# Tanh pieces for GELU, one GELU buffer, whole matmuls, and pair sums added on GpSimd, in a transformer block on one core

## The chip, the core and the metric

The kernel runs on one core of a Trainium2 chip. A core has a matmul engine (TensorE, in the profile PE, with its weight loads shown apart as PEld), a vector engine (VectorE, DVE), an engine for functions such as exp (ScalarE, ACT), GpSimd (POOL) and SyncE (SP), which here issues every DMA. Matmuls write to PSUM, eight banks of 512 float32 columns over 128 partitions; everything else lies in SBUF. The metric is the device time of one execution in microseconds. Before the change it is 1161.94 us, the median of three runs (1159.34, 1161.94 and 1164.83).

## What is computed

A block of a transformer over 2048 rows of 1024 features in bfloat16: layer norm, attention with 32 heads of width 32, a residual; layer norm, a feed-forward layer of width 3584 with GELU in its tanh form, a residual.

```python
qkv = (layernorm(x) @ wqkv).reshape(B, S, 3, H, Dh).transpose(2, 0, 3, 1, 4)   # S=2048, H=32, Dh=32
scores = einsum("bhqd,bhkd->bhqk", q, k) * Dh ** -0.5
o = einsum("bhqk,bhkd->bhqd", softmax(scores), v)
h = x + o.transpose(0, 2, 1, 3).reshape(B, S, D) @ wo                          # D=1024
g = gelu(layernorm(h) @ w1 + b1, approximate=True)                             # F=3584
out = h + g @ w2 + b2
```

## The kernel before

**Tiling.** The rows are cut into eight chunks of 256 queries (qb, or u in the feed-forward part), the heads into eight groups g of four. A *job* is one chunk and one group: eight rounds, each with 256 keys. In a round, `Att.qk` (L726) lets PE make the scores of four heads (eight matmuls of 32 rows by 256 columns, L739, four side by side in the array's rows) into two of three units of two PSUM banks, and ACT turns each unit into bfloat16 exps with one instruction of 128x1024 (L749), into one of `NR` = 6 round buffers `PT` (L384). `Job.pv` (L768) multiplies them by the values (L775, eight matmuls, four side by side in the array's columns).

**Denominators.** The sums over keys come from PE too: matmuls with a matrix of ones (L804). So that they are fewer, DVE first adds the two halves of a round's exps (the *pair sum*, L790) into one of `NS` = 2 buffers `PS` (L388); seven rounds of a job go that way, the eighth directly. When a job is done, DVE copies the bank (L827), takes reciprocals (L832) and multiplies (L838) into `OT`.

**The rest for each chunk.** `wo(u)` projects the attention's output and adds the residual (L859), `ln2(u)` normalizes (its small steps on POOL, L558 to L564), `ffn1(u)` multiplies by w1 (L896, 14 blocks of 256 features), and `ffn2(u, j)` multiplies by w2 for one half j of the columns (L930). FFN1's output is taken out of PSUM with its bias by DVE (L913), into `gT`, of which there are two, one for even and one for odd chunks (L411). When all 14 blocks are there, one ACT instruction makes GELU of all 7168 columns in place (L927). `late_q` (L646) makes later chunks' Q projections from stored normalized rows, in buffers `xq` that lie over `gT`. All of these matmuls, for which scores and values leave room, are called background (`bg`).

**Narrow and whole.** `mm` (L497) writes a matmul as four narrow ones of 32 output rows, which run side by side (mode `col`, L504), or as one whole one (mode `full`, L508). Values and denominators are always `col`, scores `row`. The background beside attention is narrow, so that between two rounds of scores the array keeps its mode; the last chunk's is whole (`tail`).

**What sets the order.** Every operation is recorded as a `Task` with its engine, an estimated cost (L457 to L465: `c_act`, `c_dve`, `MM`) and the tasks it depends on through buffers. `Graph.schedule` (L108) plays them through with these costs and fixes the order on each engine; each engine then runs its list in order, and semaphores carry the dependencies (`assign`, L209). On PE, `pick_pe` (L1103) takes scores first, then values and denominators when enough rounds wait (`PV_FORCE`, `PV_START`), else background in program order. The other engines take the lowest `prio`, then program order. All DMAs are issued by SP, in the order that the same plan gives.

The program order around the change is this (L1054 to L1082):

```python
    for g in range(2):
        if g not in EXTRA:
            proj(0, g, 1, slot(), "dve")
    late_q(1, 1, [g for g in range(2, G) if g not in EXTRA])
    wo(0)
    ln2(0)
    late_q(2, 1, range(G))
    ffn1(0)
    attention(2, [g for g in range(G) if g not in EXTRA])
    for u in range(7):
        ...
            wo(u + 1)
            ln2(u + 1)
            ffn2(u, 0)
            ffn1(u + 1)
            ffn2(u, 1)
```

Behind the loop come attention's rounds that still wait, then `ffn2(6, 0)`, `wo(7)`, `ln2(7)`, `ffn2(6, 1)`, `ffn1(7)` and `ffn2(7)`, in whole matmuls but for the first.

Of the kernel before, what the change touches and what calls it, by code (L numbers as in the profile page):

```python
# [7 lines left out]
ACT = mybir.ActivationFunctionType  # L8
# [27 lines left out]

class Task:
    __slots__ = ("eng", "fns", "occ", "lat", "deps", "prio", "kind", "mode", "left", "succ", "ready", "done",
                 "order", "inc", "flow", "value", "lane", "waits", "bytes", "acq", "rel")

    def __init__(self, eng, fns, occ, lat, prio, kind, mode):
        self.eng, self.fns, self.occ, self.lat = eng, fns, occ, lat
        self.prio, self.kind, self.mode = prio, kind, mode
        self.deps = set()
        self.succ = []
        self.left = 0
        self.ready = 0.0
        self.done = None
        self.order = None
        self.inc = False  # L50
        self.flow = None
        self.value = 0
        self.lane = None
        self.waits = ()
        self.bytes = 0
        self.acq = None
        self.rel = None


class Graph:  # L60
# [145 lines left out]
        return seqs  # L206


    def assign(self, flows, lane_flows):  # L209

        for t in self.tasks:
# [101 lines left out]
def build_kernel(nc, A_x, A_wqkv, A_wo, B_w1, B_b1, B_w2, B_b2, out):  # L313
# [7 lines left out]
    DC = D // P  # L321
    FC = F // P
    SCALE = DH ** -0.5
    EPS_BF = 1.0013580322265625e-05

    x2 = A_x[0]
# [34 lines left out]
    ident, B_ident = sb(top, "ident", [P, P], BF)  # L361
    ones32, B_ones = sb(top, "ones32", [P, 32], BF)
    one_row, B_one = sb(top, "one_row", [P, P], BF)
    b2t, B_b2t = sb(top, "b2t", [P, D], BF)
    b1b, B_b1b = sb(top, "b1b", [P, FC], BF)
    b1f, B_b1f = sb(top, "b1f", [P, FC], F32)
# [14 lines left out]
    NQ = 8  # L381
    qt_lo = top.cur
    QT, B_QT = sb(top, "QT", [P, NQ, 256], BF, NQ)
    NR = 6  # L384
    pt_lo = top.cur
    PT, B_PT = sb(top, "PT", [P, NR, 2, 2, 512], BF, 2 * NR)
    pt_hi = top.cur
    NS = 2  # L388
    PS, B_PS = sb(top, "PS", [P, NS, 4, 256], BF, NS)
    ot_lo = Area(top.cur)  # L390
    OT, B_OT_ = sb(top, "OT", [P, 3, G, 256], BF, 3 * G, 2)
# [8 lines left out]
    xnT, B_xnTt = sb(ph0, "xnT", [P, 4, DC, 512], BF, 4, 4)  # L400
    Wall, B_W = sb(ph0, "Wall", [P, 6, DC, 512], BF, 6, 4)
    NXB = 4
    xb, B_xb = sb(ph0, "xb", [P, NXB, D], BF, NXB)
    NSG = 2
    stg, B_stg = sb(ph0, "stg", [P, NSG, 512], BF, NSG)


    hch, B_hch_ = sb(ffn, "hch", [P, 4, D], BF, 8)
    B_hch = [B_hch_[2 * i:2 * i + 2] for i in range(4)]
    gt_lo = Area(ffn.cur)  # L410
    gT, B_gT = sb(ffn, "gT", [P, 2, FC, 256], BF, FC)  # L411
    xq, B_xq = [], []
    for k in range(2):
        gt_lo.cur = ffn.cur - (2 - k) * FC * 512
        h, b = sb(gt_lo, "xq%d" % k, [P, DC, 512], BF)
        xq.append(h)
        B_xq.append(b)
    hnT, B_hnT = sb(ffn, "hnT", [P, DC, 256], BF, 1, 2)

    class Rings:  # L420
# [41 lines left out]
        return (62 + n / x) / 960.0 + 0.02  # L462

    def c_act(n, ap_bias=False):
        return 0.100 + (0.093 if ap_bias else 0.0) + n / 1200.0  # L465

    def pe(fns, occ, reads=(), writes=(), kind="bg", mode="full", prio=0, after=()):
        return gr.add(E.PE, fns, occ, 0.16, reads, writes, prio, kind, mode, after)
# [25 lines left out]
        if isinstance(bank, Slot):  # L494
            t.rel = bank

    def mm(bank, lhsT, rhs, start, stop, reads, narrow, cols=(0, 512)):  # L497

        c0, c1 = cols
        occ = MM * (c1 - c0) / 512.0 + 0.003  # L500
        if narrow:
            fns = []
            for j in range(4):
                fns.append(lambda p, j=j: p.matmul(psum[32 * j:32 * j + 32, bi(bank), c0:c1], lhsT[:, 32 * j:32 * j + 32], rhs,  # L504
                                                   start=start, stop=stop, tile_position=(0, 32 * j), skip_group_check=True))
            t = pe(fns, occ, reads=reads, writes=[bb(bank)], mode="col")
        else:
            t = pe(lambda p: p.matmul(psum[:, bi(bank), c0:c1], lhsT, rhs, start=start, stop=stop),  # L508
                   occ, reads=reads, writes=[bb(bank)], mode="full")
        take(t, bank)  # L510

    def act(fn, n, reads=(), writes=(), prio=0, ap_bias=False, kind="", after=()):
# [23 lines left out]
    pool(lambda g: g.memset(ones32[:], 1.0), 0.2, writes=[B_ones])  # L536
    pool(lambda g: g.memset(one_row[:], 0.0), 0.3, writes=[B_one])
    pool(lambda g: g.memset(one_row[0:1, :], 1.0), 0.3, reads=[B_one], writes=[B_one])
    pool(lambda g: g.memset(b2t[:], 0.0), 1.0, writes=[B_b2t])


    cnt = {"ln": 0, "x": 0, "sg": 0, "ps": 0, "od": 0, "q": 0}

    def layer_norm(tiles, prio, norm="dve"):

# [213 lines left out]
    class Job:  # L759
# [8 lines left out]
        def pv(self, r, s):  # L768
            g, bank, first = self.g, self.bank, self.n == 0
            last = self.n == 7  # L770
            self.n += 1
            fns = []
            for i in range(2):
                for h in range(4):
                    fns.append(lambda p, i=i, h=h: p.matmul(  # L775
                        psum[32 * h:32 * h + 32, bi(bank), 0:256], V[:, g, 2 * r + i, 32 * h:32 * h + 32],
                        PT[:, s, h // 2, h % 2, 256 * i:256 * i + 256], start=first and i == 0, stop=last and i == 1,
                        tile_position=(0, 32 * h), skip_group_check=True))
            rd = [B_PT[2 * s], B_PT[2 * s + 1], B_V[NT * g + 2 * r], B_V[NT * g + 2 * r + 1]]
            t = pe(fns, 0.224, reads=rd, writes=[self.B_O, self.B_D] if first else [self.B_O], kind="pv", mode="col")  # L780
            take(t, bank)
            while self.sums:
                self.den(*self.sums.pop(0), False)
            if r == 7 or (self.g == 0 and self.qb < 2):
                self.sums.append((s, True))
            else:
                n = cnt["ps"] % NS
                cnt["ps"] += 1
                pairs = PT[:, s, :, :, :].rearrange("p u j c -> p (u j) c")
                dve(lambda v: v.tensor_tensor(PS[:, n, :, :], pairs[:, :, 0:256], pairs[:, :, 256:512], ALU.add), c_dve(1024, 2),  # L790
                    reads=[B_PT[2 * s], B_PT[2 * s + 1]], writes=[B_PS[n]], prio=-2)
                self.sums.append((n, False))
            if last:
                while self.sums:
                    self.den(*self.sums.pop(0), not self.sums)
                self.finish()
# [99 lines left out]
    def ffn1(u, tail=False):  # L896
        R = R2 if tail else R1
        for blk in range(FC // 2):
# [4 lines left out]
                    mm(bank, R.w1[:, s, dc, f * P:(f + 1) * P], hnT[:, dc, :], dc == 0, dc == DC - 1,  # L903
                       [R.B_w1[s]] + B_hnT, not tail, (256 * f, 256 * f + 256))
            evict1(u, 2 * blk, bank, tail)
        if not tail:
            gelu(u)

    def evict1(u, fc, bank, tail):
        h = u % 2  # L910
        B_g = B_gT[h * (FC // 2) + fc // 2]
        if not tail:
            drop(dve(lambda v: v.tensor_tensor(  # L913
                gT[:, h, fc:fc + 2, :], psum[:, bi(bank), :].rearrange("p (f c) -> p f c", f=2),
                b1f[:, fc:fc + 2].unsqueeze(2).to_broadcast([P, 2, 256]), ALU.add),
                c_dve_ps(512), reads=[bb(bank), B_b1f], writes=[B_g]), bank)
        else:
            for f in range(2):
                act(lambda a, f=f: a.activation(gT[:, h, fc + f, :], psum[:, bank, 256 * f:256 * f + 256], ACT.Gelu_apprx_tanh,
                                                bias=b1f[:, fc + f:fc + f + 1], scale=1.0),  # L920
                    256, reads=[B_ps[bank], B_b1f], writes=[B_g], ap_bias=True)

    def gelu(u):
        h = u % 2
        bs = B_gT[h * (FC // 2):(h + 1) * (FC // 2)]
        g = gT[:, h, :, :].rearrange("p f c -> p (f c)")
        gr.add(E.Activation, lambda a: a.activation(g, g, ACT.Gelu_apprx_tanh, bias=0.0, scale=1.0),  # L927
               c_act(FC * 256) + 2.6, 0.14, bs, bs, -1)

    def ffn2(u, j, wide=False, W=None, banks=None):  # L930
        R = R2 if wide else R1
# [8 lines left out]
        for t in range(2):  # L940
            bank = banks[t] if banks else slot()
            tt = 2 * u + t
            hs = 2 * (u % 2) + t
            for fc in range(FC):
                s = ws[fc // 4]
                mm(bank, gT[:, u % 2, fc, t * P:(t + 1) * P], W.w2[:, s, fc % 4, :], fc == 0, False,
                   [B_gT[(u % 2) * (FC // 2) + fc // 2], W.B_w2[s]], not wide)
            mm(bank, one_row[:, :], b2t[:, c], False, True, [B_one, B_b2t], not wide)
            o = R.next("os", R.nos)
            drop(dve(lambda v, o=o, hs=hs, bank=bank: v.tensor_tensor(  # L950
                R.ost[:, o, :], psum[:, bi(bank), :], hch[:, hs, c], ALU.add),
                c_dve_ps(512), reads=[bb(bank), B_hch[hs][j]], writes=[R.B_ost[o]]), bank)
            dma(out2[tt * P:(tt + 1) * P, c], R.ost[:, o, :], P * 1024, reads=[R.B_ost[o]], prio=0)

# [102 lines left out]
    late_q(1, 1, [g for g in range(2, G) if g not in EXTRA])  # L1057
    wo(0)
    ln2(0)
    late_q(2, 1, range(G))  # L1060
    ffn1(0)
    attention(2, [g for g in range(G) if g not in EXTRA])
    for u in range(7):
        last = u == 6
        if not last:
            wo(u + 1)
            ln2(u + 1)
            ffn2(u, 0)
            ffn1(u + 1)
            ffn2(u, 1)  # L1070
        if u == 0:
            late_q(3, 0, range(G))
        if u < 5:
            attention(u + 3, range(G))
    attention_drain()
# [56 lines left out]

    num = {t: i for i, t in enumerate(gr.tasks)}
    gr.schedule(pick_pe, pool_banks)

    sems = {e: nc.alloc_semaphore(f"f_{e.name}") for e in (E.PE, E.Activation, E.DVE, E.Pool)}
    lanes = [nc.alloc_semaphore(f"f_lane{i}") for i in range(N_LANES)]
# [69 lines left out]
```

## Time and profile before

| | |
|---|---|
| median of three runs | 1161.94 us |
| the profiled execution | 1161.92 us |
| its span, first to last instruction | 1160.1 us |
| first exp of the unbroken stretch, end of the last exp | 72.4 us, 1086.0 us |
| exps (128x1024) | 1024, of them 992 in that stretch |
| GELU instructions, table loads around them | 7 of 6.18 us, 14 of 1.28 us |
| pair sums on DVE (L790) | 434 of 0.69 us |
| mean granted TensorE clock | 0.985 |

The profile is one execution. A line of a group gives the source line, engine, operation, output<-input with shapes and the number of instructions; after the first bar the group's busy time in us and the mean of one in ns (where neighbours overlap, the mean counts the overlap twice and the busy time does not); after the second the time that the engine stood idle before these instructions, with what ended it. A timeline line gives start and length in us, engine, source line, operation and number merged. "x52" on PE are single narrow matmuls, so 13 groups of four. Two shares in the middle of the run are nearly full at once: PE 94% and ACT 91% of the span; DVE is at 60% and POOL at 4%.

### The profile page before, as it was taken

The page shows a single profiled execution, that of the slowest core. Times are in us where ns is not written, and L with a number is a line of the kernel's source. Part 1 is how long each engine was busy: PE and PEld are TensorE (multiplying, and loading weights), DVE is VectorE, ACT ScalarE, POOL GpSimd, SP SyncE. Part 2 cuts the span into 40 slices and gives each one's busy share as a digit, 9 for nine tenths or more (in the row PEclk, how much of TensorE's full clock was granted, in tenths as well). Part 3 has the DMA queues.
Part 4 walks back from the last instruction along what each step waited for, and adds up shares of the span by engine and source line. Part 5 has one row for each costly group of instructions (what it writes and reads, how often), then busy time and mean ns, then how long its engine had stood idle before and what let it go on. Part 6 is the DMA issues. An engine that isn't in the chain of part 4 may idle for free.

```text
span 1160.1 us, 54760 instructions
## 1 busy us (share of the span) xinstructions
PE 1091.6 (94%) x25756; PEld 638.1 (55%) x25762; DVE 697.4 (60%) x1119; ACT 1052.5 (91%) x1096; POOL 44.4 (4%) x108
## 2 busy tenths in 40 slices
PE   8999999998998899999998999999999999887998
PEld 6655455554456456544574565466457544563484
DVE  7656676676775566467665664766476457663500
ACT  4879999999999989999999999999999999989540
POOL 3200000000100100001000000100010000000100
PEclk9999999999999999999999999999999999898999
DMA  6920200046445455646458556565576658673480
GB/s 180 233 84 3 66 20 4 3 115 207 115 139 153 132 181 167 198 142 193 131 164 256 167 166 211 150 200 153 164 230 171 206 169 247 179 208 102 145 264 19
DMA packets 265412, 174.99 MB, mean 151 GB/s; under 512 B 26849, under 2 KB 260321, under 8 KB 264418
## 3 DMA queue, kind: packets, MB, share of 16 engines
q1 hardware_dynamic: 265186, 171.48, 50.3%
q8 instruction: 202, 3.31, 1.2%
q14 instruction: 24, 0.20, 0.1%
HBM read 160.97 MB, written 10.49 MB: 148 GB/s over the span
## 4 chain that ended last, share of the span: by engine, by line
PE 66%; ACT 23%; DVE 6%; issue 2%; DMA 2%; POOL 0%; SPq 0%; DVEq 0%; POOLq 0%
PE ps L504 38%; ACT PT L749 19%; PE ps L739 11%; PE ps L775 6%; PE ps L508 6%; PE ps L804 4%; ACT gT L927 3%; DVE PS L790 2%; DVE gT L913 1%; DMA a_w2r<-in_B_w_dram 1%; PE ps L968 1%; PE ps L574 1%; DMA hch<-in_A_x_dram 1%; ACT L927 1%; DVE a_ost L950 0%
## 5 line engine op out<-in xcount | busy, mean ns | idle before, releaser
L749 ACT ACTIVATE PT<-ps 128x1024 bf16<-128x1024 f32 x1024 | 959.8, 1037 | 39.9 <-PE ps L739 34.7
L790 DVE TENSOR_TENSOR PS<-PT 128x1024 bf16<-128x1024 bf16 x434 | 289.6, 688 | 185.7 <-PE ps L804 152.6
L739 PE MATMUL ps<-QT,KT 32*128 32x256 bf16 x4096 | 206.1, 275 | 24.7 <-ACT PT L749 21.5
L504 PE MATMUL ps<-hnT,a_w1r 128*32 128x256 bf16 x6272 | 216.6, 275 | 11.3 <-issue 6.1
L504 PE MATMUL ps<-a_w2r,gT 128*32 128x512 bf16 x2912 | 196.5, 385 | 9.6 <-ACT gT L927 8.1
L775 PE MATMUL ps<-PT,V 128*32 128x256 bf16 x4096 | 185.1, 277 | 5.2 <-issue 3.6
L504 PEld LDWEIGHTS ps<-hnT,a_w1r 128*32 128x32 bf16 x6272 | 154.2, 96 | 58.9 <-issue 46.0
L739 PEld LDWEIGHTS ps<-QT,KT 32*128 32x128 bf16 x4096 | 61.2, 92 | 181.0 <-ACT PT L749 126.9
L804 PE MATMUL ps<-PS,ones 128*32 128x256 bf16 x1736 | 125.2, 279 | 4.5 <-issue 1.9
L775 PEld LDWEIGHTS ps<-PT,V 128*32 128x32 bf16 x4096 | 108.2, 98 | 32.3 <-issue 7.0
L832 DVE RECIPROCAL OD<-OD 128x128 f32<-128x128 f32 x128 | 117.9, 936 | 0.5
L504 PEld LDWEIGHTS ps<-a_w2r,gT 128*32 128x32 bf16 x2912 | 69.1, 97 | 78.3 <-issue 25.8
L913 DVE TENSOR_TENSOR gT<-ps,b1f 128x512 bf16<-128x512 f32 x98 | 67.1, 685 | 73.1 <-PE ps L504 72.5
L504 PE MATMUL ps<-xnT,Wall 128*32 128x512 bf16 (+1 forms) x1536 | 93.1, 363 | 2.1 <-issue 0.7
L504 PE MATMUL ps<-Wall,xnT 128*32 128x256 bf16 x2048 | 70.5, 274 | 1.7 <-ACT xnT L581 0.7
L804 PEld LDWEIGHTS ps<-PS,ones 128*32 128x32 bf16 x1736 | 47.2, 97 | 27.9 <-DVE PS L790 9.7
L504 PE MATMUL ps<-a_w1r,OT 128*32 128x512 bf16 x896 | 59.8, 390 | 2.0 <-DVE OT L838 0.6
L504 PEld LDWEIGHTS ps<-Wall,xnT 128*32 128x32 bf16 x2048 | 50.3, 96 | 14.5 <-issue 7.6
L504 PEld LDWEIGHTS ps<-xnT,Wall 128*32 128x32 bf16 x1536 | 37.7, 97 | 34.4 <-issue 13.2
L827 DVE COPY OD<-ps 128x512 f32<-128x512 f32 x63 | 43.2, 686 | 4.5 <-PE ps L775 3.4
L558 POOL CAST mvb<-mv 128x2 bf16<-128x2 f32 (+1 forms) x24 | 5.3, 223 | 1048.0 <-DVE mv L555 1045.4
L504 PE MATMUL ps<-xq,a_w1r 128*32 128x512 bf16 x672 | 44.4, 381 | 0.6 <-DMA a_w1r<-in_A_wqkv_dram 0.4
(76 smaller groups left out, 616.0 us busy)
## 6 DMA issues: line engine op xcount, KB each, us to landing
a_w2r<-in_B_w_dram SPq DMA_DIRECT2D x105, 512.0 KB, 6.3
a_w1r<-in_B_w_dram SPq DMA_DIRECT2D x98, 512.0 KB, 4.5
a_w1r<-in_A_wo_dram SPq DMA_DIRECT2D x32, 512.0 KB, 4.4
b_w1r<-in_B_w_dram SPq DMA_DIRECT2D x14, 512.0 KB, 4.4
a_w1r<-in_A_wqkv_dram SPq DMA_DIRECT2D x11, 512.0 KB, 4.6
xrb<-in_A_x_dram SPq DMA_DIRECT2D x16, 256.0 KB, 4.4
Wall<-in_A_wqkv_dram SPq DMA_DIRECT2D x16, 256.0 KB, 5.3
hch<-in_A_x_dram SPq DMA_DIRECT2D x16, 256.0 KB, 4.5
```

Of the source, the lines that this page charges most:

```text
L504: fns.append(lambda p, j=j: p.matmul(psum[32 * j:32 * j + 32, bi(bank), c0:c1], lhsT[:, 32 * j:32 * j + 32], rhs, start=start, stop=stop, ...
L508: t = pe(lambda p: p.matmul(psum[:, bi(bank), c0:c1], lhsT, rhs, start=start, stop=stop), occ, reads=reads, writes=[bb(bank)], mode="full")
L574: t = pe(lambda p, dc=dc: p.transpose(psb[:, bi(bank), dc * P:(dc + 1) * P], src_ap[:, dc * P:(dc + 1) * P], ident[:]), 0.064, reads=[B_sr ...
L739: return p.matmul(psum[:, 2 * us[h // 2] + h % 2, 256 * i:256 * i + 256], KT[32 * h:32 * h + 32, g, k0:k0 + P], QT[32 * h:32 * h + 32, qs, :],
L749: act(lambda a, u=u, k=k: a.activation(PT[:, s, k, :, :], psum[:, 2 * u:2 * u + 2, :], ACT.Exp, bias=0.0, scale=SCALE), 1024, reads=[B_ps[ ...
L775: fns.append(lambda p, i=i, h=h: p.matmul(psum[32 * h:32 * h + 32, bi(bank), 0:256], V[:, g, 2 * r + i, 32 * h:32 * h + 32], PT[:, s, h // ...
L790: dve(lambda v: v.tensor_tensor(PS[:, n, :, :], pairs[:, :, 0:256], pairs[:, :, 256:512], ALU.add), c_dve(1024, 2), reads=[B_PT[2 * s], B_ ...
L804: fns.append(lambda p, h=h, rhs=rhs, i=i: p.matmul(psum[32 * h:32 * h + 32, bi(bank), 256:512], ones32[:, :], rhs, start=False, stop=last, ...
L827: t = dve(lambda v: v.tensor_copy(OD[:, o, :, :], psum[:, bi(bank), :]), c_dve_ps(512), reads=[self.B_O, self.B_D], writes=B_O + B_D, prio=-1)
L832: dve(lambda v, c=c: v.reciprocal(OD[:, o, 1, c], OD[:, o, 1, c]), 0.93, reads=[B_D[k]], writes=[B_D[k]], prio=1)
L913: drop(dve(lambda v: v.tensor_tensor(gT[:, h, fc:fc + 2, :], psum[:, bi(bank), :].rearrange("p (f c) -> p f c", f=2), b1f[:, fc:fc + 2].un ...
L927: gr.add(E.Activation, lambda a: a.activation(g, g, ACT.Gelu_apprx_tanh, bias=0.0, scale=1.0), c_act(FC * 256) + 2.6, 0.14, bs, bs, -1)
```

## The change

1. **GELU from Tanh, in pieces.** Instead of one GELU instruction per chunk, every two blocks of FFN1 (1024 columns of `gT`) are a piece: DVE squares (`tensor_tensor`), adds a constant and multiplies by x (`scalar_tensor_tensor`), ACT takes Tanh with the rest of the constants as its scale, DVE adds 1 and multiplies by x. `gT` then holds twice GELU, so the bias row of FFN2 is 2 and the eviction multiplies by 0.5. Chunk 7 keeps the old instruction.
2. **One GELU buffer.** `gT` is single; chunk 7 has its own over `PT`. In program order FFN1 of chunk u+1 comes behind both halves of FFN2 of chunk u. FFN2 waits for the last bias add of its chunk (`biased`). The space goes to `NR` = 7 and `NS` = 4, and to two work buffers `uu`.
3. **Whole matmuls.** After planning, `merge_tiles` looks at each run of column-mode tasks on PE; if a run has only `mm` tasks, their four narrow matmuls become one whole one.
4. **GpSimd adds pair sums.** Rounds 0 and 1, 2 and 3, 4 and 5 of a job: GpSimd adds the second pair sum to the first, and PE makes one denominator step for both. Round 6 and 7 stay as they were, and so do the first two jobs.
5. **Smaller things.** `late_q(2)` and `late_q(3)` both come ahead of `ffn1(0)`; the planner's cost of an ACT instruction falls by 0.027 us; the lead's normalized tiles `xb` lie over the end of `V`.

```diff
-    NR = 6
+    NR = 7
...
-    NS = 2
+    NS = 4
...
-    gT, B_gT = sb(ffn, "gT", [P, 2, FC, 256], BF, FC)
+    gT, B_gT = sb(ffn, "gT", [P, FC, 256], BF, FC // 2)
+    NU = 2
+    uu, B_uu = sb(ffn, "uu", [P, NU, 1024], BF, NU)
...
-        return 0.100 + (0.093 if ap_bias else 0.0) + n / 1200.0
+        return 0.073 + (0.093 if ap_bias else 0.0) + n / 1200.0
...
+    def merge_tiles(self):
+
+        run = []
+        for t in self.seqs[E.PE] + [None]:
+            if t is not None and t.mode == "col":
+                run.append(t)
+                continue
+            if all(x.whole is not None for x in run):
+                for x in run:
+                    x.fns, x.mode = [x.whole], "full"
+            run = []
...
-                self.sums.append((n, False))
+                if r == 6 or (self.g == 0 and self.qb < 2):
+                    self.sums.append((n, False))
+                elif r % 2 == 0:
+                    self.half = n
+                else:
+                    k = self.half
+                    pool(lambda e: e.tensor_tensor(PS[:, k, :, :], PS[:, k, :, :], PS[:, n, :, :], ALU.add), 2.2,
+                         reads=[B_PS[k], B_PS[n]], writes=[B_PS[k]], prio=-1)
+                    self.sums.append((k, False))
...
-        gr.add(E.Activation, lambda a: a.activation(g, g, ACT.Gelu_apprx_tanh, bias=0.0, scale=1.0),
-               c_act(FC * 256) + 2.6, 0.14, bs, bs, -1)
+    def gelu(u, k):
...
+        dve(lambda v: v.tensor_tensor(w, g, g, ALU.mult), c_dve(1024, 2), reads=b, writes=[B_uu[i]], prio=1)
+        dve(lambda v: v.scalar_tensor_tensor(w, w, C2, g, ALU.add, ALU.mult), c_dve(1024), reads=b + [B_uu[i]], writes=[B_uu[i]], prio=1)
+        act(lambda a: a.activation(w, w, ACT.Tanh, bias=0.0, scale=KT2), 1024, reads=[B_uu[i]], writes=[B_uu[i]], prio=-1)
+        dve(lambda v: v.scalar_tensor_tensor(g, w, 1.0, g, ALU.add, ALU.mult), c_dve(1024), reads=b + [B_uu[i]], writes=b, prio=1)
...
-            mm(bank, one_row[:, :], b2t[:, c], False, True, [B_one, B_b2t], not wide)
+            row, B_row, half = (one_row, B_one, 1.0) if u == 7 else (two_row, B_two, 0.5)
+            mm(bank, row[:, :], b2t[:, c], False, True, [B_row, B_b2t], not wide)
...
-    late_q(2, 1, range(G))
+    late_q(2, 0, range(G))
+    late_q(3, 1, range(G))
     ffn1(0)
     attention(2, [g for g in range(G) if g not in EXTRA])
-    for u in range(7):
-        last = u == 6
-        if not last:
-            wo(u + 1)
-            ln2(u + 1)
-            ffn2(u, 0)
-            ffn1(u + 1)
-            ffn2(u, 1)
-        if u == 0:
-            late_q(3, 0, range(G))
+    for u in range(6):
+        wo(u + 1)
+        ffn2(u, 0)
+        ln2(u + 1)
+        ffn2(u, 1)
+        ffn1(u + 1)
         if u < 5:
             attention(u + 3, range(G))
```

## The prediction

> **What bounds the kernel now.** I began with the page's first lines: the busy shares of the engines.
>
> ```profile
> span 1160.1 us, 54760 instructions
> ...
> PE 1091.6 (94%) x25756; PEld 638.1 (55%) x25762; DVE 697.4 (60%) x1119; ACT 1052.5 (91%) x1096; POOL 44.4 (4%) x108
> ```
>
> PE and ACT are both nearly full, so neither share decides. The stages do. The timeline shows ACT's exps almost without a break from 72.4 us on, the last ending at 1086.0; before that the stage loads and fills, and after it PE works alone for 74.1 us (1160.1 - 1086.0). So the span is a lead (72.4), an ACT stage (1013.6) and a PE tail (74.1). The groups of ACT in the window of the middle stage divide it:
>
> ```profile
> L749 ACT ACTIVATE PT<-ps 128x1024 bf16<-128x1024 f32 x992 | 928.3, 1037 | 25.7 <-PE ps L739 20.5 <-PE ps L775 0.8
> L927 ACT ACTIVATE gT<-gT 128x7168 bf16<-128x7168 bf16 x7 | 43.2, 6178 | 0.1
> L927 ACT ACT_TABLE_LOAD x7 | 9.0, 1283 | 0.1
> L749 ACT ACT_TABLE_LOAD x7 | 9.0, 1283 | 0.1
> ```
>
> The mean of 1037 ns overlaps its neighbours; what an exp costs is 928.3/992 = 0.936 us, a round (two exps) 1.872. GELU takes 43.2 + 18.0 = 61.2, and the rest, 1013.6 - 928.3 - 61.2 = 24.1, is idle: ACT waiting for score matmuls (L739), that is, for PE. Why PE is late is in PE's timeline, three rounds in which it does nothing but scores and FFN1:
>
> ```profile
> 453.46 0.40 PE L739 MATMUL ps<-QT,KT 32*128 32x256 bf16 x8
> 453.79 1.60 PE L504 MATMUL ps<-hnT,a_w1r 128*32 128x256 bf16 x52
> 455.32 0.40 PE L739 MATMUL ps<-QT,KT 32*128 32x256 bf16 x8
> 455.65 1.71 PE L504 MATMUL ps<-hnT,a_w1r 128*32 128x256 bf16 x56
> 457.29 0.40 PE L739 MATMUL ps<-QT,KT 32*128 32x256 bf16 x8
> ```
>
> The 52 narrow matmuls are 13 groups of four that run side by side. With 13 groups the scores come 1.86 us apart, with 14 they come 1.97 apart: a group of 256 columns costs about 0.108, and scores with their two mode changes 1.86 - 13 x 0.108 = 0.45. A round is thus 0.45 + 0.108 x groups (512 columns count as two groups), and 13 groups just fill ACT's 1.872. This is the measure for everything below.
>
> **The change, part by part.**
>
> *Tanh pieces on ACT.* The listing of the changed program has 49 Tanh of 128x1024, no table load between exps, and 43 of the 49 ahead of the last exp. An operation of that size costs 0.936 (the exp row). The ACT stage loses 61.2 and gains 43 x 0.936 = 40.2: **-21.0**.
>
> *ACT's idle 24.1.* I counted, in both listings, the groups that PE has between scores and summed the longer of PE's and ACT's time, from round 16 on. Round by round, before gives 1016.9 against 987.9 of ACT alone (29.0 idle); with two rounds taken together, 1003.0 (15.1). The trace's 24.1 lies 65% of the way. After gives 20.2 and 4.7 over its 966.0, so by the same place 14.8: **-9.3**. The reason is that PE has less in its rounds: 860 us instead of 914, of which the pair adds take 184 groups (583 to 399, 20 us).
>
> *PE's tail.* The other 34 us are not gone. Behind the last scores the old listing has 652 groups of projections and FFN, the new one 963: 195 groups of FFN1 and 112 + 4 of FFN2 of chunk 6 now stand there. One GELU buffer forces this: FFN1 of chunk u+1 comes behind both halves of FFN2 of chunk u, no longer between them. At 311 x 0.108 this adds **+33.5**, in a stage where nothing lies beside it.
>
> *GELU of chunk 6 in the tail.* All seven pieces now run there. A piece is three DVE operations. The first is a pair add like L790's; the other two take 1024 elements through a form that the trace lacks. Bounds: L790's 0.69, if it also runs two elements at a time, and from L838 (256 elements, 0.42) to L790 (512 steps, 0.69) 1.05 ns a step, so 1.22 one at a time. I take 1.15 (1.22 less the 0.07 by which neighbours overlap), as a two-operation form is no plain add. A piece is then 0.65 + 2.3 = 2.95. From the last pair sum DVE has 3 us of finishing work, 12 bias adds of 0.61 (L913's 0.685 less the overlap) and seven pieces, 31 us, and starts some 3 us behind the last scores; FFN2 needs the last piece about 27 us behind them (FFN1's 195 groups 21.1, a bias add 0.7, then 24 of FFN2's first 28 matmuls, 5.2). PE stands **+7** (0, if the form runs at L790's pace).
>
> *DVE and GpSimd in the attention.* These rows carry the addition's price:
>
> ```profile
> L790 DVE TENSOR_TENSOR PS<-PT 128x1024 bf16<-128x1024 bf16 x434 | 289.6, 688 | 185.7 <-PE ps L804 152.6 <-ACT PT L749 28.6 <-PE ps L739 2.0
> ...
> L539 POOL MEMSET b2t<- 128x1024 bf16 x1 | 1.0, 957 | 0.0
> ```
>
> GpSimd writes 128x1024 in 0.96; an add reads two such streams too: 0.96 to 3 x 0.96 = 2.9. I take 2.2, which the new code books for it. And GpSimd does not have its path to itself:
>
> ```profile
> 732.05 0.69 DVE L790 TENSOR_TENSOR PS<-PT 128x1024 bf16<-128x1024 bf16 x1
> ...
> 732.12 0.67 POOL L558 CAST mvb<-mv 128x2 bf16<-128x2 f32 x1 [93.13 <-DVE mv L555]
> ...
> 302.54 0.19 POOL L558 CAST mvb<-mv 128x2 bf16<-128x2 f32 x1 [256.26 <-DVE mv L555]
> ```
>
> The same cast takes 0.19 alone and 0.67 beside a pair sum, ending 0.05 after it. So the two exclude each other; whether DVE waits as long for a GpSimd add, no row shows. In the new order 21 jobs (eight rounds each) hold 42 GELU pieces. By the groups' means less the overlap, DVE works 14.6 us in such a job (10.3 of it with two SBUF inputs), GpSimd 3 x 2.2 = 6.6, ACT 16.85. Packed perfectly, 10.3 + 6.6 fill the job exactly and cost nothing; if all of GpSimd's time is added to DVE's, a job takes 21.2, 4.4 too much, 92 in all. Engines run in order, so perfect is out of reach; DVE's other 4.3 us and its idle 2.2 can cover most. I take 1 us a job: **+21**. Behind a late DVE operation stand bias adds and pair sums; PE waits for the first's bank and for the sums' denominators, and the next scores are queued behind those on PE. The new order leaves 3 rounds between a pair's scores and its denominator 45 times, 4 rounds 123 times; by the rows a round's exps end about 2.8 us behind the scores, sum and add take 2.9, so 3 rounds (5.6) have no slack.
>
> The Trainium skill (SBUF — State Buffer, "Who interferes with whom") says that a DVE operation with two SBUF inputs and a GpSimd operation that reads SBUF exclude each other, whichever starts first, for a whole instruction. The rows above show one direction; by the rule both hold, and this part would lean to its upper end, not to nothing.
>
> The same skill (GPSIMD Engine Reference, "Performance versus the Vector engine") gives about 2.6 cycles at 1.2 GHz for an element of a two-input operation, an estimate of 2.2 us for the add; no row here shows one.
>
> *Whole matmuls.* A whole 128x256 costs 24.6/224 = 0.110 in the tail, four narrow ones 0.108:
>
> ```profile
> L508 PE MATMUL ps<-hnT,b_w1r 128*128 128x256 bf16 x224 | 24.6, 273 | 0.0
> ```
>
> 1,725 are joined, +-3.5, taken as nothing; the mode changes stay as many, since only runs between other modes are joined. *Costed at nothing:* seven score buffers and four sum buffers (they remove DVE's wait of 152.6 for L804, idle time of an engine with room; next late is the exp, 28.6); the output's scaled add (32 of 0.69, one PSUM input as L950's; 19 more on DVE if twice as long); two memsets of 0.2 ahead of b2t's, under which the warm-up waits 2.7 already; the Q projections moved earlier (two loads of 1 MB, 8 weight blocks and 16 stores pass the Q loads on SP's queue; under attention, and a weight block late by 3.9 us, as the chain shows at 300 us, is the price if not); the new wait for the last bias add, placed where PE reaches it after other work.
>
> **Sum.** 1160.1 - 21.0 - 9.3 + 33.5 + 7 + 21 = 1191.3 of span; the profiled execution took 1161.92, 1.8 more, and the median of the runs is 1161.94, so 1193.
>
> **Rivals.** (1) *The path costs nothing*: adds fall between DVE's operations, 1193 - 21 = 1172, between 1158 (no stall in the tail, 7 less idle) and 1178. For it: in the 41 jobs without pieces DVE works about 9.8 of 15. (2) *DVE becomes the bound*: half or more of the 4.4 is paid, 1172 + 46 to 92 = 1218 to 1264; an add of 2.9 does it alone. (3) *Faster: ACT is never idle.* PE's 860 us are 106 below ACT's 966; if slack in one round makes up for excess in the next, idle is 0, and if the two-input form runs at L790's pace the path is free and the tail has no stall: 1161.9 - 21.0 - 24.1 + 33.5 = 1150. It decides once idle and stalls together stay under 6 us. Against it: the order is fixed by booked costs, and 24 us were lost so before. (4) *The change does not do what it says*: matmuls joined, loads gone, adds moved, and all given back: within 0.5%.
>
> **Chances.** Measurement tells 0.5% (5.8 us) from no change. Forecast 0.42; rival 1 0.25 (0.13 of it within 1156 to 1168); rival 2 0.14; rival 3 0.17; rival 4 0.02. Slower 0.42 + 0.12 + 0.14 = 0.68, same 0.15, faster 0.17. The range leaves out the ends of rivals 2 and 3: 1145 to 1238; the forecast's own is 1178 to 1215.
>
> **What would show it.** No table loads between exps and 992 exps at 0.936; the last exp near 1076; PE for about 115 us behind it, with a gap at FFN2 of chunk 6; pair sums (L790's successor) above 0.69 or GpSimd adds above 2.2 where they meet; PE waits on denominators. Wrong if adds take 1 us, if the pieces run at 0.69 each, or if ACT's idle time grows without such waits.

## The result and the profile after

The changed kernel takes 1230.26 us (median of four runs, 1228.74 to 1233.08) against 1162.16 for the kernel before on the same chip: a ratio of 1.0581, 95% interval 1.0546 to 1.0615. It is slower by 68 us, where 31 were forecast. The page's first lines:

```profile
span 1227.0 us, 43302 instructions
...
PE 1071.4 (87%) x19791; PEld 602.6 (49%) x19843; DVE 1003.7 (82%) x1266; ACT 1032.3 (84%) x1124; POOL 469.9 (38%) x296
```

No engine is nearly full any more. PE fell from 94 to 87% and ACT from 91 to 84%, while DVE rose from 60 to 82%: each now waits for another. Divided as the prediction did, with the start of the unbroken exps (the 33rd), the end of the last exp and the end of the span as borders:

| | lead | ACT stage (ACT idle in it) | from last exp to PE's last matmul | span |
|---|---|---|---|---|
| before | 72.4 | 1013.6 (24.1) | 71.1 | 1160.1 |
| after | 69.0 | 1042.7 (80.8) | 112.2 | 1227.0 |

The tail is 41.1 longer, as forecast (40.5). The stage should have become 9 shorter and became 29 longer. ACT's groups in the window of the stage:

```profile
L774 ACT ACTIVATE PT<-ps 128x1024 bf16<-128x1024 f32 x992 | 923.2, 1072 | 55.9 <-PE ps L764 55.3
L968 ACT ACTIVATE uu<-uu 128x1024 bf16<-128x1024 bf16 x42 | 44.5, 1059 | 30.2 <-DVE uu L967 29.9
```

The table loads are gone. ACT's idle time has two parts: it waits 55 us for scores, where it waited 20.5 before, and, which is new, 30 us with a Tanh in hand for DVE's second GELU step (L967). The groups of DVE and GpSimd on the page say why DVE is late:

```profile
L823 POOL TENSOR_TENSOR PS<-PS 128x1024 bf16<-128x1024 bf16 x186 | 421.2, 2264 | 600.4 <-DVE PS L815 600.4
L815 DVE TENSOR_TENSOR PS<-PT 128x1024 bf16<-128x1024 bf16 x434 | 415.1, 966 | 69.9 <-ACT PT L774 52.8
...
L967 DVE SCALAR_TENSOR_TENSOR uu<-uu,gT 128x1024 bf16<-128x1024 bf16 x49 | 73.5, 1501 | 0.1
```

The pair sum, the same instruction as L790 before, went from 289.6 to 415 us of busy time. The mean of 0.966 is no common value. I set each DVE operation against the times of the GpSimd adds: the 310 pair sums under which no add runs take 0.679 (median), the 124 that meet one take 1.687 on average and up to 2.65. L966 goes from 0.679 to 1.337, the two longer GELU steps from 1.21 to 1.96 and 1.82. Operations that read PSUM do not change: the bias add L947 takes 0.680 alone and 0.679 beside an add, the copy L860 0.684 and 0.687. The add itself takes 2.12 undisturbed and 2.264 on average.

These means mix two orders, and it matters who starts first. Where the add did, the DVE operation is late by the time that both overlap less 0.13 us, in the median of the 119 pair sums and of the GELU steps alike. Where DVE did (11 of L966, 10 of L967, 9 of L969 and 5 pair sums), its operation keeps its own time, and the add pays: up to 3.05 instead of 2.12. The prediction had left open whether DVE waits as long for a GpSimd add as the cast had waited for DVE; it does.

The timeline from 437 to 444 us shows what one such meeting does (lines of other work left out):

```profile
437.11 2.12 POOL L823 TENSOR_TENSOR PS<-PS 128x1024 bf16<-128x1024 bf16 x1 [3.56 <-DVE PS L815]
437.27 2.51 DVE L815 TENSOR_TENSOR PS<-PT 128x1024 bf16<-128x1024 bf16 x1 [0.24 <-PE ps L837]
...
439.70 1.21 DVE L967 SCALAR_TENSOR_TENSOR uu<-uu,gT 128x1024 bf16<-128x1024 bf16 x1
...
440.28 0.40 PE L764 MATMUL ps<-QT,KT 32*128 32x256 bf16 x8
...
440.95 1.06 ACT L968 ACTIVATE uu<-uu 128x1024 bf16<-128x1024 bf16 x1 [1.05 <-DVE uu L967]
441.28 0.69 DVE L860 COPY OD<-ps 128x512 f32<-128x512 f32 x1
...
442.12 1.89 PE L528 MATMUL ps<-a_w1r,OT 128*128 128x512 bf16 x8 [1.45 <-DVE OD L860]
```

GpSimd starts first, so the pair sum stands until the add ends at 439.23 and ends 0.55 after it: 1.83 us late, of 1.96 that they overlap. Behind it on DVE are L967, for which ACT waits 1.05, and the copy L860, which frees a bank for which PE waits 1.45. On PE the next scores are queued behind that matmul; they start at 443.94, 3.66 after the last ones at 440.28, where the rounds of before were 1.86 apart.

The Trainium skill (SBUF — State Buffer, "Who interferes with whom") says that a DVE operation with two SBUF inputs contends with a GpSimd operation that reads SBUF, not with one that only writes, and that whoever comes second waits for the whole instruction. These lines agree (1.83 us waited beside an add of 2.12; 0.679 beside an add and 0.680 alone for an operation with one PSUM input); whether writes are free is tried below.

The waits of the whole execution name the same ways, ACT behind PE's scores and behind DVE's GELU step, and PE behind the add and behind DVE's bias adds (of the 56.5 us some 27 lie in the tail, where ACT has little else to do):

```profile
ACT PT L774 <- PE ps L764: 62.9, 74, 5.3
ACT uu L968 <- DVE uu L967: 56.5, 29, 8.8
...
PE ps L837 <- POOL PS L823: 15.3, 18, 1.9
PE ps L525 <- DVE gT L947: 15.2, 28, 1.7
```

PE's waits can cost more than their own length, because its granted clock (1 is full speed) falls after them. One case, on PE's timeline:

```profile
417.19 0.29 PE L837 MATMUL ps<-PS,ones 128*32 128x256 bf16 x4 [1.55 <-POOL PS L823]
419.48 0.41 PE L837 MATMUL ps<-PS,ones 128*32 128x256 bf16 x4 [2.00 <-DVE PS L815]
...
420.52 2.51 PE L525 MATMUL ps<-hnT,a_w1r 128*32 128x256 bf16 x44
```

After the two waits the clock is 0.5 from 419.4 to 422.8 us, and 11 groups of FFN1 take 2.51 us, 0.228 each instead of 0.108. The stage has nine such stretches, 37.5 us together; in the 3.4 us ahead of each, PE was busy for 0.09 to 0.44 of the time. Half of that, 18.8 us, is the most that they can have added to the stage, if PE set the pace throughout. Before, the stage had 30.7 us of them.

### The profile page after: what moved, and what is told of

Same layout as the page of the kernel before. It is cut to its first block, busy times and chain, and to the rows that moved or that the text cites. A ratio compares the mean times of both kernels' runs of the same rounds, so it can differ in the third digit from the quotient of the medians.

```text
span 1227.0 us, 43302 instructions
## 1 busy us (share of the span) xinstructions
PE 1071.4 (87%) x19791; PEld 602.6 (49%) x19843; DVE 1003.7 (82%) x1266; ACT 1032.3 (84%) x1124; POOL 469.9 (38%) x296
## 4 chain that ended last, share of the span: by engine, by line
ACT 33%; DVE 32%; PE 29%; issue 4%; DMA 1%; POOL 0%; SPq 0%; DVEq 0%
ACT PT L774 32%; DVE PS L815 13%; PE ps L525 11%; PE ps L531 6%; PE ps L528 5%; DVE uu L967 4%; PE ps L764 4%; DVE gT L947 3%; DVE OD L865 3%; PE ps L800 2%; DVE gT L969 2%; DVE uu L966 2%; PE ps L837 1%; ACT uu L968 1%; DVE OT L871 1%
## 5 line engine op out<-in xcount | busy, mean ns | idle before, releaser
L823 POOL TENSOR_TENSOR PS<-PS 128x1024 bf16<-128x1024 bf16 x186 | 421.2, 2264 | 600.4 <-DVE PS L815 600.4
L815 DVE TENSOR_TENSOR PS<-PT 128x1024 bf16<-128x1024 bf16 x434 | 415.1, 966 | 69.9 <-ACT PT L774 52.8
L525 PE MATMUL ps<-hnT,a_w1r 128*32 128x256 bf16 x3416 | 123.1, 284 | 17.9 <-DVE gT L947 13.1
L525 PE MATMUL ps<-a_w2r,gT 128*32 128x512 bf16 x1860 | 130.5, 381 | 5.3 <-DVE a_ost L992 2.3
L525 PEld LDWEIGHTS ps<-hnT,a_w1r 128*32 128x32 bf16 x3416 | 88.8, 100 | 40.8 <-issue 23.1
L968 ACT ACTIVATE uu<-uu 128x1024 bf16<-128x1024 bf16 x49 | 51.9, 1059 | 56.8 <-DVE uu L967 56.5
L528 PE MATMUL ps<-hnT,a_w1r 128*128 128x256 bf16 x714 | 89.7, 274 | 5.7 <-DVE gT L947 3.1
L947 DVE TENSOR_TENSOR gT<-ps,b1f 128x512 bf16<-128x512 f32 x98 | 66.6, 680 | 15.5 <-PE ps L525 10.5
L528 PEld LDWEIGHTS ps<-hnT,a_w1r 128*128 128x128 bf16 x714 | 65.0, 98 | 27.0 <-issue 14.4
L967 DVE SCALAR_TENSOR_TENSOR uu<-uu,gT 128x1024 bf16<-128x1024 bf16 x49 | 73.5, 1501 | 0.1
L969 DVE SCALAR_TENSOR_TENSOR gT<-uu,gT 128x1024 bf16<-128x1024 bf16 x49 | 69.8, 1424 | 0.0
L528 PE MATMUL ps<-a_w2r,gT 128*128 128x512 bf16 x239 | 59.5, 380 | 6.3 <-issue 2.1
L860 DVE COPY OD<-ps 128x512 f32<-128x512 f32 x63 | 43.2, 686 | 12.4 <-PE ps L800 11.3
```

Source lines behind the costliest of these rows:

```text
L528: t.whole = lambda p: p.matmul(psum[:, bi(bank), c0:c1], lhsT, rhs, start=start, stop=stop, skip_group_check=True)
L823: pool(lambda e: e.tensor_tensor(PS[:, k, :, :], PS[:, k, :, :], PS[:, n, :, :], ALU.add), 2.2, reads=[B_PS[k], B_PS[n]], writes=[B_PS[k]] ...
L947: t = dve(lambda v: v.tensor_tensor(g[:, fc:fc + 2, :], psum[:, bi(bank), :].rearrange("p (f c) -> p f c", f=2), b1f[:, fc:fc + 2].unsquee ...
L967: dve(lambda v: v.scalar_tensor_tensor(w, w, C2, g, ALU.add, ALU.mult), c_dve(1024), reads=b + [B_uu[i]], writes=[B_uu[i]], prio=1)
L969: dve(lambda v: v.scalar_tensor_tensor(g, w, 1.0, g, ALU.add, ALU.mult), c_dve(1024), reads=b + [B_uu[i]], writes=b, prio=1)
```

## The experiments

**Theory P**: GpSimd's reads hold DVE, DVE's late operations hold PE and ACT. **Rival L**: an add makes its denominator late by its own 2 us, and PE waits for that. **Rival D**: DVE is too full with the GELU pieces' 3.1 us, whatever GpSimd does.

### 1. Small adds

```diff
-  pool(lambda e: e.tensor_tensor(PS[:, k, :, :], PS[:, k, :, :], PS[:, n, :, :], ALU.add), 2.2,
+  pool(lambda e: e.tensor_tensor(PS[:, k, :, 0:4], PS[:, k, :, 0:4], PS[:, n, :, 0:4], ALU.add), 2.2,
```

> The changed kernel with every order kept, but each GpSimd add does 4 of each 256 columns (16 of 1024, so the denominators are wrong): the wait chain stays, the time that GpSimd holds its path goes. Theory P (DVE operations with two SBUF inputs stand still while a GpSimd add runs): pair sums go back to 0.68 us each, ACT's idle time in its stage falls from about 75 to 15 to 25 us, and the time to 1165 to 1185. Rival D (the GELU pieces alone fill DVE, the adds matter little): 1215 to 1230, GELU phases as slow as now. Rival L (denominators come late because an add takes 2.1 us, without any hold): also 1165 to 1185, so this run does not part P from L.

1142.67 us, ratio 0.9775 (0.9744 to 0.9806): faster than the kernel before, with the GELU pieces all there. The span is 1141.0; the stage takes 955.2 with 5.5 of ACT idle, the tail 113.4. D falls. The price of the adds is 1227.0 - 1141.0 = 86 us in the profiled executions; by the two ratios, each against the kernel before in its own series of runs, it is 0.0806 of 1162, 94. The half-clock stretches are part of it, with 18.8 at most, as this run has none. That the time lies below what P and L expected shows that the rest of the change gains more than I had reckoned.

### 2. The same time on GpSimd, writes only

```diff
-  pool(lambda e: e.tensor_tensor(PS[:, k, :, :], PS[:, k, :, :], PS[:, n, :, :], ALU.add), 2.2,
+  pool([lambda e: e.memset(scr[:], 1.0), lambda e: e.memset(PS[:, k, :, :], 1.0)], 2.2,
```

> As the changed kernel, but instead of the add GpSimd writes twice 128x1024 (constants, so the denominators are wrong), which takes about as long (2 x 0.96 us) and reads nothing from SBUF. Denominators come as late as with the add. Theory P, if the hold is by GpSimd's reads: pair sums at 0.68 us, time 1165 to 1190. Theory P, if writing holds the path as well: pair sums stay near 0.97 us in the mean, time 1215 to 1235. Rival L (lateness of the denominators is the cost): time 1215 to 1235 with pair sums at 0.68 us.

1143.63 us, 0.9786 (0.9759 to 0.9813), span 1141.3. GpSimd still ends some 1.9 us behind the second pair sum, and PE's denominators wait for it as in the changed kernel. The page's groups of DVE's pair sum and of GpSimd:

```profile
L816 DVE TENSOR_TENSOR PS<-PT 128x1024 bf16<-128x1024 bf16 x434 | 297.1, 687 | 151.0 <-ACT PT L775 117.9
L824 POOL MEMSET scr<- 128x1024 bf16 x186 | 177.5, 954 | 596.1 <-DVE PS L816 596.1
...
L824 POOL MEMSET PS<- 128x1024 bf16 x186 | 177.5, 954 | 0.0
```

The pair sums are back at 0.687 beside 355 us of GpSimd writing, and nothing of the 86 us is left. So it is the reading that holds DVE (P), and the lateness of the denominators costs nothing by itself (L falls).

Both programs have the changed kernel's order on PE, ACT and DVE, so the 86 us can be placed job by job (16 exps each). From the first unbroken exp on, the 23 jobs with Tanh pieces are together 67.9 us longer than in this run, 2.95 each, and the 39 without are 20.5 longer, 0.52 each.

### 3. The adds without the GELU steps

```diff
-  dve(lambda v: v.tensor_tensor(w, g, g, ALU.mult), ...
+  dve(lambda v: v.tensor_tensor(w[:, 0:16], g[:, 0:16], g[:, 0:16], ALU.mult), ...
```

The two other steps likewise; Tanh reads `g` instead of `w`.

> The changed kernel with every order kept and full adds on GpSimd, but the three DVE operations of a GELU piece do 16 of 1024 columns (GELU is left out; Tanh on ACT stays). Theory P: port demand of a job falls from 10.3 + 6.6 to about 5 + 6.6 of 15 us, so most of the loss goes: 1165 to 1190, with pair sums still above 0.68 us in the mean (0.8 to 1.0) because adds still hold the path. Rival D: 1155 to 1170, and pair sums at 0.68 us.

1178.05 us, 1.0067 (1.0018 to 1.0115), span 1179.5, stage 991.0. The pair sums among DVE's groups:

```profile
L815 DVE TENSOR_TENSOR PS<-PT 128x1024 bf16<-128x1024 bf16 x434 | 399.3, 928 | 121.6 <-ACT PT L774 100.5 <-PE ps L837 18.9
```

The time is what theory P expected. The pair sums are held almost as before (0.928), but DVE has room. Of the 86 us 38 remain (1179.5 - 1141.3; 33 by the ratios); the other 48 need both, the hold and a DVE that has no time to make it up. So D was wrong as a rival and right as a part of the cause. The 38 take for granted that without the hold the GELU steps cost nothing, as ACT's idle time of 4.7 in run 2 suggests; no run leaves out both.

### 4. Narrow matmuls again

```diff
-    gr.merge_tiles()
```

> The changed kernel without joining narrow matmuls into whole ones, nothing else. By the rows (0.108 narrow, 0.110 whole for 256 columns) both theories say no change: within 4 us of the changed kernel, 1226 to 1234. If whole matmuls help beside scores, it is slower than 1236.

1241.12 us, 1.0628 (1.0588 to 1.0668), against 1.0581 for the change; the span is 9.7 longer (1236.7). That would make the whole matmuls worth 5 us by the ratios and 10 by the spans, but the two intervals overlap, so this run alone doesn't show it; run 8 isolates them.

### 5. All pair sums straight to PE

```diff
-                if r == 6 or (self.g == 0 and self.qb < 2):
+                if True:
```

> The changed kernel without GpSimd adds: every pair sum has its own denominator step on PE again, and the plan is made anew. Theory P (DVE's operations with two SBUF inputs stand still under an add): the hold's 86 us go; the new order has 231 more groups of 256 columns behind the last scores, 231 x 0.108 = 25 us, and about 2 us more in the rounds: 1227 - 86 + 27 = 1168 of span, 1.00 to 1.01 of the time before. Rival D (GELU pieces alone fill DVE): 1215 or more, 1.045 and up.

1176.02 us, 1.0099 (1.006 to 1.0139). The plan is made anew here: the denominators take 186 groups of PE more (434 of pair sums instead of 248), and the plan leaves 1194 behind the last scores instead of 963. The stage takes 962.3, the tail 141.2. The ratio is what P expected, and D falls again. Two of the change's parts now show apart: the stage is 51 shorter than before the change, the tail 70 longer.

### 6. The planner's old ACT cost

```diff
-        return 0.073 + (0.093 if ap_bias else 0.0) + n / 1200.0
+        return 0.100 + (0.093 if ap_bias else 0.0) + n / 1200.0
```

> The changed kernel with the planner's cost of an ACT instruction at 0.100 again (0.073 in the change), nothing else; one GELU buffer and the program order stay. If the one buffer puts FFN1 of chunk 6 behind the last exp, as the prediction said, PE's tail stays at 112 us. If it is the planner's cost (rounds planned 0.054 us shorter hold one group less each), the tail is 71 to 75 us as before the change, the rounds hold 311 groups more, and, with the hold of the adds still there, the time is 1187 to 1212, 1.02 to 1.045 of the time before.

1231.52 us, 1.0566 (1.0514 to 1.0617): not faster, so the expectation was wrong. Its listing has 652 groups behind the last scores, exactly as many as the kernel before, with one GELU buffer. So it was not the buffer that moved 311 groups into the tail but, in this program, this number: with 0.073 the planner thinks that ACT is quicker, and gives PE less to do between scores. (The number does it only together with the rest of the plan: in run 10, with the adds planned on DVE, 0.110 leaves 961 groups there.) The tail is back at 70.3. But the stage went from 1042.7 to 1087.2, its idle time from 80.8 to 110.6. PE's clock is at half for 78.5 us of this stage, 37.5 in the changed kernel.

### 7. Both undone

```diff
-    MM = 0.2195
+    MM = 0.211
...
-        return 0.073 + (0.093 if ap_bias else 0.0) + n / 1200.0
+        return 0.110 + (0.093 if ap_bias else 0.0) + n / 1200.0
...
-                if r == 6 or (self.g == 0 and self.qb < 2):
+                if True:
```

> A version meant to beat both: Tanh pieces, one buffer, whole matmuls; no GpSimd adds; planner costs set so that rounds are filled (ACT 0.110, 512 columns 0.211 instead of 0.2195). The order has 652 groups behind the last scores, as before the change. From the 1168 of the version without adds: 542 groups less in the tail (-58), no GELU stall in it (-7), rounds 30 us longer: 1133, 0.965 to 0.985 of the time before. If the pieces' DVE work is a bound of its own (rival D), 1.00 or more.

1142.79 us, 0.9815 (0.9777 to 0.9852): Tanh pieces, one buffer and whole matmuls without GpSimd's adds, with planner costs that leave 652 groups behind the last scores. Stage 997.6, tail 71.3, span 1139.1. Against run 5 the tail gives back 69.9 and the stage takes 35.3: without the hold the planner's costs are worth 35 us. The ratio is inside the expected range; the span is 6 us above the 1133 of the sum.

### 8. The kernel before with whole matmuls

Before, with `merge_tiles` and `t.whole` added and nothing else; the order on each engine is that of before.

> The kernel before with whole matmuls alone (runs of background between scores joined, order kept). By the rows, 0.110 for a whole one against 0.108 for four narrow ones: no change, 0.996 to 1.004 of the time before. If fewer instructions or mode changes help beside scores, below 0.995.

1146.55 us, 0.984 (0.9794 to 0.9885). I had expected no change. The span is 1147.4, 12.7 shorter, in an execution that was the slowest of its four; the ratio makes it 19 us, 13 to 24. Set exp by exp against before, the 33rd exp comes 3.75 us earlier and the 993rd 12.74, in some fourteen steps of 0.5 to 1.6 us, with 3.8 lost again near 770 us, and not by a steady gain per round; the tail is the same. Nearly all the steps lie where PE of before stood with nothing to wait for, and the loss where PE of this run did. PE's waits on "issue", in before:

```profile
PE ps L504 <- issue: 7.0, 8, 1.4
...
PE ps L775 <- issue: 3.6, 2, 1.8
PE ps L804 <- issue: 1.9, 3, 1.1
PE ps L739 <- issue: 1.8, 2, 1.2
```

and with whole matmuls:

```profile
PE ps L818 <- issue: 4.3, 4, 1.8
...
PE ps L753 <- issue: 1.2, 2, 0.8
PE ps L789 <- issue: 0.7, 2, 0.5
```

The page's row of the queue that loads instructions (queue, packets, MB, share), before and with whole matmuls:

```profile
q8 instruction: 202, 3.31, 1.2%
q8 instruction: 153, 2.51, 0.9%
```

14.3 us of standing became 6.2, which is 8 of the 12.7. In the same way PE of the changed kernel stands 10.0 us on "issue" and that of run 4 19.1, which is 9 of the 9.7 between their spans. The program executes 42328 instructions instead of 54760 and loads 2.51 MB of them instead of 3.31. That PE waited for instructions to be loaded fits the rows, and a stretch of the changed kernel's tail: FFN1 of chunk 6 stays narrow there, because values and denominators stand in the same run of column-mode tasks, and further on chunk 7's is whole.

```profile
1120.54 7.23 PE L525 MATMUL ps<-hnT,a_w1r 128*32 128x256 bf16 x254 [1.11 <-issue]
1128.44 3.67 PE L525 MATMUL ps<-hnT,a_w1r 128*32 128x256 bf16 x127 [0.68 <-issue]
1132.92 3.67 PE L525 MATMUL ps<-hnT,a_w1r 128*32 128x256 bf16 x127 [0.81 <-issue]
...
1174.25 24.62 PE L531 MATMUL ps<-hnT,b_w1r 128*128 128x256 bf16 x224
```

After every 127 narrow matmuls, each with its weight load, or twice that PE stands 0.7 to 1.1 us. From 1120.54 to 1137.30, 508 narrow matmuls, 127 groups, take 16.76: 0.132 a group, where the whole ones take 0.110. No run here changed the loading alone, so the cause of these gaps is likely and not shown; that whole matmuls save them is.

### 9. The old ACT cost with small adds

Run 6 with the diff of run 1.

> The changed kernel with the planner's ACT cost at 0.100 again and GpSimd's add cut to 4 of each 256 columns (the denominators then miss most of the second pair's sum). With full adds the cost took the tail from 112 to 70 us and the time stayed, because the stage grew by 44. If the hold on DVE is what turned PE's extra work in the stage into time, the gain now appears: lead 69, PE's rounds 895 and ACT's 1024 x 0.920 + 49 x 0.94 give a stage of 965 to 985, tail 71, span 1105 to 1125, ratio 0.95 to 0.97, some 15 to 35 us below the small adds with the order of the change. If PE's work in the stage costs its own time whatever the hold, span is 1141 again, ratio 0.978, with a stage near 1000.

1125.28 us, 0.9674 (0.9629 to 0.9718), span 1124.1: stage 981.1, tail 70.3. Against run 1 the tail gives back 43.1 and the stage takes 25.9, a gain of 17 at the upper end of what P said (1105 to 1125). Under the hold the same number gave nothing: 41.9 back from the tail for 44.4 in the stage (run 6). So 26 of the 44 come without any hold, and 18 go with it: run 6 put the work, and the last seven GELU pieces with it, into a stage in which DVE was late already.

### 10. The adds on DVE

```diff
-                    pool(lambda e: e.tensor_tensor(PS[:, k, :, :], PS[:, k, :, :], PS[:, n, :, :], ALU.add), 2.2,
+                    dve(lambda v: v.tensor_tensor(PS[:, k, :, :], PS[:, k, :, :], PS[:, n, :, :], ALU.add), c_dve(1024, 2),
```

and the ACT cost at 0.110.

> The two-by-two adds kept whole, but as DVE operations of the size of a pair sum (0.69 us), and the planner's ACT cost at 0.110, which leaves 961 groups of 256 columns behind the last scores, as many as the changed kernel has. If only GpSimd's reads hold DVE, 186 adds of 0.69 fit into DVE's idle time and the pair sums stay at 0.69: lead 69, stage 960 to 990, tail 112, span 1140 to 1170, ratio 0.98 to 1.01. If the later denominators or the shared sum buffers are what delays the stage, span is above 1200 as in the changed kernel.

1173.66 us, 1.0079 (1.0053 to 1.0106), span 1171.7, some 2 above the expected band; stage 982.4 and tail 113.4 as expected, the lead 3 longer. DVE's groups of pair sums and of the adds:

```profile
L815 DVE TENSOR_TENSOR PS<-PT 128x1024 bf16<-128x1024 bf16 x434 | 293.4, 681 | 61.9 <-ACT PT L774 48.3 <-PE ps L837 9.5
L823 DVE TENSOR_TENSOR PS<-PS 128x1024 bf16<-128x1024 bf16 x186 | 128.0, 688 | 4.1
```

The sum buffers are shared and the denominators come after two adds as in the changed kernel, and the span is 55 us shorter. What differs is where the adds run, the planner's cost that keeps the tail alike, and the order that the plan makes of both. On DVE the 186 adds take 128 us, 0.69 each. On GpSimd they took more of DVE than that: over the stage DVE is busy 915.6 us in the changed kernel and 750.8 in run 2, which is 165 us or 0.89 for each add.

## Why the prediction was wrong

The likeliest case said 1193 and 1230 came. Its steps:

- **The path, "I take 1 us a job: +21".** This is the step that failed. Runs 1 and 2 put the price at 86. The bounds were right: the upper one, 4.4 us in a job with GELU pieces, held, and 2.95 came, in 23 jobs where 21 were counted. Two things were wrong in the choice. I let DVE's 4.3 us of unaffected work and its idle 2.2 swallow most of the hold, but the order is fixed and each engine runs in turn, so an add meets whatever DVE happens to do, and a late L967 or L860 goes straight on to ACT and PE. And I gave the 41 jobs without pieces nothing; the 39 measured paid 20.5. The cast that waited for a pair sum had shown exclusion in one direction, and the rule of the Trainium skill that the prediction cites said both; leaning on it gave rival 2, *DVE becomes the bound*, which had 0.14. Its condition came true (2.95 of the 4.4 paid, 67.9 us), but that its 1218 to 1264 holds the result is partly luck: its base of 1172 was 31 us too high, and it had no price for the jobs without pieces either. Nor is DVE a bound by itself; it is busy for 88% of the stage (915.7 of 1042.7).
- **Tanh on ACT and the idle time, -21.0 and -9.3.** Too small. In run 1, without the hold, the stage took 955.2 instead of 1013.6, -58.4: ACT busy 949.7 instead of 989.5 (-39.8), idle 5.5 instead of 24.1 (-18.6). The price of 0.936 for an operation was the fault. It was a mean over a stretch in which some exps had waited and so did not overlap their neighbours; in run 1 the 992 exps and 42 Tanh cost 0.919 each, and back to back an exp costs 0.920, as one line of ACT's timeline of the changed kernel has it, 29.44 / 32:

```profile
149.90 29.44 ACT L774 ACTIVATE PT<-ps 128x1024 bf16<-128x1024 f32 x32 [1.41 <-PE ps L764]
```

- **PE's tail, +33.5 and +7.** The sum was right (41.1 against 40.5), in part by luck. The 311 groups were there, but not because "one GELU buffer forces this": the planner's ACT cost did it, which I had listed among the smaller things (run 6). And the stall of 7 for the last GELU piece did not come, PE waited 1.1 for DVE's L947 in this tail; instead FFN1's narrow groups, with the gaps described under run 8, took 26 us instead of 21, time in which DVE got further: its last GELU step ended 7.8 us after FFN1, and PE had work till then.
- **Whole matmuls, nothing.** They gain 12.7 us of span in run 8 (19 by the ratio); the 9.7 of run 4 fit, but lie within the noise. I compared their pace, where there is none to gain (0.110 and 0.108), and not the number of instructions.
- **The prices of single operations** were right: the two-operation form 1.22 (1.215 measured), GpSimd's add 2.2 (2.12), the piece's first step 0.69.

With what was measured the sum reads: 1160.1 - 58.4 (stage without the hold) + 42.3 (tail, run 1) - 3.1 (lead) = 1141, + 86 = 1227. It closes by construction, as the 86 is the difference of the two spans. Some 8 (run 4) to 13 us (run 8) of the gain in stage and lead belong to the whole matmuls.

For the part of run 6 one thing stays open: why the stage grew by 44 when 34 us of matmuls and seven pieces came back to it. ACT is busy 14.6 us longer and idle 29.8 longer. It waited for DVE's GELU steps hardly more than in the changed kernel (33 us against 30) and longer before exps, for PE above all (80.9 against 55.9). PE's half-clock stretches can explain 20.5 of the growth at most (39.3 of lost time instead of 18.8). No engine is over 90% busy, and the rest is not explained.

## What to carry to other kernels

Before work moves from DVE to GpSimd, count on both engines the operations that read two SBUF operands: each meeting costs the later one the rest of the other's instruction, whichever engine it is, and in a kernel with fixed orders this goes on to whoever waits behind. Take the price of an operation from a stretch in which it runs back to back, not from a mean over a stage. A planner's cost constant is a change like any other: here one number moved 311 groups from one stage to another. Of all versions that compute everything, run 7 (0.9815) and run 8 (0.984) are the fastest; their intervals overlap.

## What the runs showed of the hardware

- A GpSimd add that reads SBUF stops a DVE operation with two SBUF inputs that starts behind it for all but 0.13 us of the overlap (0.679 alone, 1.687 on average and 2.65 at most beside adds of 2.12); a DVE operation that starts first is not slowed, and the add waits (3.05 at most). Two GpSimd writes of 0.95 each hold nothing (0.687). Operations with one PSUM input are free (0.680 and 0.679), but a `tensor_scalar` with a single SBUF tensor as input (L593) is not: 0.542 alone, 1.22 and 2.35 in the two cases that started behind an add.
- `scalar_tensor_tensor` of 128x1024 in bfloat16 with both tensors in SBUF takes 1.215 us, nearly twice the 0.68 of `tensor_tensor` on operands of the same size.
- Long runs of narrow matmuls (32 output rows, four side by side) lose 0.7 to 1.1 us at intervals, 0.132 a group in all against 0.110 for a whole matmul of the same columns.
- PE's granted clock was 0.5 for 3.4 us or more after stretches of 3.4 us in which PE was busy for less than half of the time (0.09 to 0.44 in the changed kernel's stage); a group of 256 columns then took 0.228 instead of 0.108.
